# Splitting one x load, dropping ten filler matmuls and moving one transpose to another PSUM bank in a 2:4-sparse matmul on one core

## The chip, the cores and the metric

The kernel runs on one core of a Trainium2 chip. Its time is the device time of one execution in microseconds (us). Three executions of the kernel before took 232.72, 232.92 and 232.72 us, median 232.72 us. A profiled execution beside them took 232.79 us.

The engines named below are TensorE (PE, with its weight loads shown as PEld), VectorE (DVE), ScalarE (ACT), GpSimd (POOL), and SyncE (SP), which here only issues DMAs. ACT issues DMAs as well.

## The reference

```python
B, S, D = 16, 512, 1024              # x: [B,S,D], w: [D,D], b: [D], all bf16
wg = w.reshape(D // 4, 4, D)         # groups of four rows
mag = abs(wg)
thr = second largest of the four magnitudes, per group and column
wp = (wg * (mag >= thr)).reshape(D, D)
return einsum("bsd,df->bsf", x, wp) + b
```

Of every four neighbouring rows of a weight column, only the two largest magnitudes are kept. Then 8192 tokens of 1024 features are multiplied with the pruned 1024x1024 weights and a bias is added.

## The kernel before

**Tiles.** The 8192 tokens are 64 tiles of 128. Tiles 0 to 6 are "packed" tiles (`NPK = 7`): their first half of the features is loaded as it lies in memory (`load_x`, lines 107 to 112), transposed on PE (`transpose`, line 197, instructions on line 202), copied out of PSUM by ACT (`copy_xt`, line 205, token `C`), and multiplied with pieces of the pruned weights as soon as each piece is ready (`mm_piece`, line 221, instructions on line 236, token `M`). All other tiles come through transposing DMAs (lines 118, 244, 416) and use whole pruned weights (`nat`, line 248, instructions on line 250).

**Pruning.** The weights are pruned in six pieces. Piece 0 is 256 columns of the upper half of the rows. It arrives in two loads, one on SP's queue and one on ACT's, and DVE makes it in fifteen instructions from `abs0a` to `mult0h` before further ones follow. The first product `M5.0g` needs the transposed and copied tile 5 (`C5a`) and the first 128 columns of half of piece 0 (`mult0g`).

**Order.** Nothing at the start is left to a scheduler. The loads are issued in the order of lines 124 to 136. The work of PE, DVE, ACT and SP is four lists of tokens (lines 274 to 296), which `run` writes out, each engine in exactly its own list's order. On PE the list starts `T5a T3a T4a F4 T6a M5.0g M3.0g M5.0h M3.0h M4.0g M4.0h T2a`: transposes of tiles 5, 3, 4, four filler matmuls, the transpose of tile 6, six short groups of products, the transpose of tile 2. A little later come `T0a` and `T1a`.

**Fillers.** `filler` (line 143, instructions on line 145) writes matmuls of constant ones into a bank that nobody reads. Lines 409 and 410 put six of 512 columns and fourteen of 128 columns ahead of everything on PE.

**Banks.** PSUM has eight banks: two in `psum_t`, six in `psum_o`. Transposes use the two of `psum_t` in turn, so a transpose waits for the ACT copy of the last but one (`needs`, line 317). Tile 4 alone is transposed in a bank of `psum_o` and waits for no copy. The fillers' bank is also one of `psum_o`.

**Queues and semaphores.** The DMAs get eight semaphores in turn, so a DMA waits until the one eight places before it has landed. SP's queue before: half of piece 0, x tiles 3 and 4 in one load of 256 KB, piece 1, x tile 2, x tiles 0 and 1, piece 2, piece 3, piece 4, then the transposing load `xlead` of tiles 7 to 11, and then the spreads of pruned weights (`wp_nat`). ACT's queue: the other half of piece 0, x tile 5, x tile 6.

**End.** The last `LATE = 6` tiles (58 to 63) store their two halves separately; the last one stores four parts.

Of the kernel before, what the change touches and what calls it, by code (L numbers as in the profile page):

```python
# [10 lines left out]
def kernel(  # L11
# [8 lines left out]
    P = 128  # L20
    bf16 = mybir.dt.bfloat16
    fp32 = mybir.dt.float32
# [10 lines left out]
    FH = 512  # L33
# [8 lines left out]
    STG = 8  # L42
    SOLO = 6
    GROUPS = ((0, 3), (3, 6), (6, 7))
    LATE = 6
    sizes = (4, 8, 8, 8, 8, 8, 8)
    batches = []
    t0 = NPK + LEAD
# [11 lines left out]
    psum_t = ctx.enter_context(tc.tile_pool(name="psum_t", bufs=2, space=bass.MemoryType.PSUM))  # L60
    psum_o = ctx.enter_context(tc.tile_pool(name="psum_o", bufs=6, space=bass.MemoryType.PSUM))
# [12 lines left out]
    def pe(i):  # L74
        return seq("pe", i)
# [4 lines left out]
    def act(i):  # L80
        return seq("act", i)

    def sp(i):
        return seq("sp", i)
# [10 lines left out]
    def tokens(dram, t):  # L95
        a, b_ = next(s for s in GROUPS if s[0] <= t < s[1])
        return dram[a * P:b_ * P].rearrange("(p t) k -> p t k", p=P), t - a
    bias_sb = const.tile([P, Dout], bf16)

    def issue(eng, out_, in_):  # L100
        q = nc.sync if eng == "sp" else nc.scalar
        return seq(eng, q.dma_start(out_, in_))  # L102

    def load_w(g, c0, c1, ma=0, mb=4, eng="sp"):
        issue(eng, w_sb[:, g, ma:mb, c0:c1], wv[:, g, ma:mb, c0:c1])

    def load_x(ta, tb, eng="sp"):
        xs = const.tile([P, tb - ta, HK], bf16, name=f"x_{ta}")
        xv, n = tokens(xf, ta)
        issue(eng, xs[:], xv[:, n:n + tb - ta, :HK])  # L110
        for t in range(ta, tb):
            x_sb[t] = xs[:, t - ta, :]
# [13 lines left out]
    load_x(5, 6, "act")  # L126
    load_x(SOLO, SOLO + 1, "act")
    act(nc.scalar.activation(spark[:], nc.const_aps.tensor(1.0, [P, 1], bf16), Act.Abs))
    load_x(3, 5)
    load_w(0, 256, 512)  # L130
    load_x(2, 3)
    load_x(0, 2)
# [10 lines left out]
    def filler(n, rep=1):  # L143
        for _ in range(n):
            pe(nc.tensor.matmul(warm_ps[:, :rep * P], lhsT=nc.const_aps.tensor(1.0, [P, P], bf16),  # L145
                                rhs=nc.const_aps.tensor(1.0, [P, rep * P], bf16), start=True, stop=True))
# [4 lines left out]
    def spread(g, c0, c1, ks=range(4), eng="sp"):  # L151
        for k in ks:
            issue(eng, wp_nat[:, 4 * g + k, c0:c1], wp[32 * k:32 * k + 32, g, :, c0:c1])
# [39 lines left out]
                self.tt(wp[:, self.g, ms, self.c0 + ca:self.c0 + cb], self.w[:, ms, ca:cb], self.mag[:, ms, ca:cb], Alu.mult)  # L193

    xpk = {}

    def transpose(t):
        xg = x_sb[t].rearrange("p (q m) -> p m q", m=4)
        bank = psum_o.tile([P, FH], fp32, name="ps") if t == 4 else psum_t.tile([P, FH], fp32, name="tp")
        tp = bank[:].bitcast(bf16)[:, :FH].rearrange("p (m q) -> p m q", m=4)  # L200
        for m in range(4):
            pe(nc.tensor.transpose(tp[:, m, :], xg[:, m, :], ident[:]))  # L202
        xpk[t] = tp
# [49 lines left out]
    def open_solo(h):  # L253
        ps = ps_open[(NPK, "h", h)] = psum_t.tile([P, FH], fp32, name="tp")
        nat(xnat[NPK], ps[:], h * FH, (h + 1) * FH, 0, 4, last=3)
# [11 lines left out]
    def stage(key):  # L267
        solo = key[1] == "h"
        q, h, at = (pair_of[key[0]], key[2], int(key[0] != SOLO)) if solo else (key[0], key[1] // 2, key[1] % 2)
        if (q, h) not in staged:  # L270
# [2 lines left out]

    order = {
# [28 lines left out]
    def all_of(tok, i):  # L303
        return [tok + x for x in halves.get(i, ("",))]

    def split_tok(tok):
        k = tok[-1] if tok[-1] in "xyabuvstghjk" else ""
        return (tok[:-1] if k else tok), k

    transposed = []  # L310

    def needs(eng, tok):
        base, k = split_tok(tok)
        if tok[0] == "C":
            return ["T" + tok[1:]]
        if tok[0] == "T":
            return ["C" + transposed[-2]] if tok != "T4a" and len(transposed) > 1 else []
        if tok[0] == "F":
            return []
        if tok[0] == "W":  # L320
            g, h = map(int, tok[1:4].split("."))
            return [n for i, pc in enumerate(pieces) if pc[0] == g and pc[1] // FH == h for n in all_of(f"mult{i}", i)]
        if tok[0] in "XYZ":
            return ["A0h1"] if tok == "Y1" else []
        if tok[0] == "A":
            return ["X0", f"W0.{tok.split('h')[1]}"] + ([f"U{NPK}h{tok[-1]}"] if tok[1] == "3" else [])
        if tok[0] == "E":
            return ["X0", f"W0.{tok[1]}"]
        if tok[0] == "U":
            t, h = map(int, tok[1:].split("h"))  # L330
            if t == NPK:
                return [f"E{h}"]
            return [f"M{t}.{x}" for i, pc in enumerate(pieces) if pc[0] == 0 and pc[1] // FH == h for x in all_of(str(i), i)]
        if base[0] == "M":
            t, i = base[1:].split(".")
            return [f"C{t}a", f"mult{i}{k}"]
        if tok[0] == "S":
            q, n = map(int, tok[1:].split("b"))
            return [f"M{t}.{x}" for i, pc in enumerate(pieces) if pc[0] == 0 and pc[1] // CW == n
                    for t in pairs[q] for x in all_of(str(i), i)]  # L340
        i, step = base[-1], base[:-1]
        before = {"abs": [], "hi": ["abs"], "lo": ["abs"], "t1": ["hi"], "t2": ["lo"],
                  "thr": ["t1", "t2"], "mask": ["thr", "hi", "lo"], "mult": ["mask"]}[step]
        out_ = []
        for b_ in before:
            if b_ in ("t1", "thr") and int(i) in SPLIT:
                out_ += [b_ + i + s for s in {"j": "j", "k": "k", "g": "j", "h": "k"}.get(k, "jk")]
            elif b_ == "t2":
                out_.append(b_ + i)
            elif b_ in ("abs", "hi", "lo") and int(i) in by_rows:  # L350
                out_ += [b_ + i + k] if step in ("hi", "lo") else [b_ + i + s for s in "ab"]
            else:
                out_.append(b_ + i + (k if b_ == "mask" else ""))
        return out_

    def emit(eng, tok):
        base, k = split_tok(tok)
        if tok[0] == "T":
            transpose(int(tok[1:-1]))
            if tok != "T4a":  # L360
                transposed.append(tok[1:])
        elif tok[0] == "F":
            filler(int(tok[1:]))
        elif tok[0] == "W":
            g, h = map(int, tok[1:4].split("."))
            spread(g, h * FH, (h + 1) * FH, {"": range(4), "p": range(2), "q": range(2, 4)}[tok[4:]], eng)
        elif tok[0] == "Z":
            load_w(1, 512, 1024)
            sp(nc.sync.dma_start(bias_sb[:], b.partition_broadcast(P)))
        elif tok[0] == "X":  # L370
            xnat.update(load_lead(int(tok[1:])))
        elif tok[0] == "Y":
            xnat.update(load_low(int(tok[1:])))
            if tok == "Y1":
                tc.add_manual_dep(tails["sp"].ins, ends["A0h1"].ins.name, SYNC, reason="let the spread of the lower weights pass")
        elif tok[0] == "E":
            open_solo(int(tok[1:]))
        elif tok[0] == "U":
            t, h = map(int, tok[1:].split("h"))
            stage((t, "h", h))  # L380
        elif tok[0] == "A":
            open_nat(*map(int, tok[1:].split("h")))
            ends[tok] = tails["pe"]
        elif tok[0] == "C":
            copy_xt(int(tok[1:-1]))
        elif tok[0] == "M":
            mm_piece(*map(int, base[1:].split(".")), part[k], cols.get(k))
        elif tok[0] == "S":
            stage(tuple(map(int, tok[1:].split("b"))))
        else:  # L390
            i = int(base[-1])
            if i not in p:
                p[i] = Piece(i)
            if eng == "act":
                p[i].abs_act()
            else:
                p[i].do(base[:-1], part.get(k, slice(0, 4)), half.get(k, slice(0, 2)), cols.get(k))
# [9 lines left out]
            assert moved, queues  # L407

    filler(6, 4)
    filler(14)  # L410
    run({eng: order[eng].split() for eng in order})

    def load_nat(ta, tb):
# [39 lines left out]
    def store(eng, t, o, c0=0, c1=Dout):  # L453
        issue(eng, rows(t)[:, c0:c1], o[:, c0:c1])
# [25 lines left out]
    for bi, (tb, nb) in enumerate(batches):  # L480
        if bi:
            load_batch(bi + 1)
        for j in range(nb):
            t = tb + j
            xt = xnat[t]
            o = outp.tile([P, Dout], bf16, name="o")
            if t == NT - 1:
                for n, (c0, c1) in enumerate(((0, FH), (FH, FH + CW), (FH + CW, Dout - P), (Dout - P, Dout))):
                    ps = psum_o.tile([P, FH], fp32, name="ps")
# [3 lines left out]
            else:  # L493
# [4 lines left out]
                for h in range(2):  # L498
                    evac(o, pss[h][:], h * FH, (h + 1) * FH)
                    if t >= NT - LATE:  # L500
                        store("act", t, o, h * FH, (h + 1) * FH)
                if t < NT - LATE:
                    store("act", t, o)
# [30 lines left out]
```

## Time and profile before

| | |
|---|---|
| median of three runs | 232.72 us |
| profiled execution | 232.79 us, span 231.0 us |
| PE busy | 226.1 us (98%) |
| PE busy from 6.29 to 19.39 us (products with pieces) | 13.10 of 13.10 us |
| PE idle ahead of its first transpose | 0.38 us, until x tile 5 is there |
| DVE idle ahead of its first instruction | 3.58 us, until the first weights are there |
| fillers (line 145) | 24 instructions |
| transposes on PE (line 202) | 28 instructions |
| mean traffic of the DMAs from 4.95 to 6.29 us | 346 GB/s, share of the 16 engines 1.11 |

Times are counted from the span's start. In the timeline a row merges instructions of one line that follow one another: start, length, engine, line, operation, output and inputs, number, and in brackets the idle time ahead of it with what ended it. The length of a matmul row runs to the end of the last matmul's passage through the array; the next matmul starts well before that. The chain of waits goes back from the last instruction, each step to what released it.

### The profile page before, as it was taken

What the parts mean: (1) busy time and instruction counts of PE and PEld (TensorE: products, weight loads), DVE (VectorE), ACT (ScalarE), POOL (GpSimd) and SP (SyncE); (2) the same over time, 40 slices, a digit from 0 to 9 for tenths busy, and PEclk for the clock granted to TensorE, in tenths of its full rate; (3) what the DMA queues carried; (4) which work ended last, traced back from release to release, by engine and by line L of the source; (5) the groups of instructions that cost most, each with busy time, mean ns of one, the idle gap of its engine ahead of it and who ended that gap; (6) DMA issues with size and microseconds to landing.
All of it is one profiled execution on the core that took longest, in us unless ns stands there. A gap on an engine that the chain in (4) does not pass through costs nothing.

```text
span 231.0 us, 2846 instructions
## 1 busy us (share of the span) xinstructions
PE 226.1 (98%) x1142; PEld 110.9 (48%) x1162; DVE 107.8 (47%) x196; ACT 13.3 (6%) x26; POOL 17.6 (8%) x15
## 2 busy tenths in 40 slices
PE   7999999999999999999999999999999999999995
PEld 4985444444444444444444444444444444444443
DVE  3999787844424424424424424423423423433434
ACT  3665100000000000000000000000000000000000
POOL 1000199700000000000000000000000000000000
PEclk9999999999999999999999999999999999999999
DMA  6999799997399222991159821796129952122122
GB/s 210 296 216 238 190 208 224 290 282 266 134 239 272 82 91 72 229 287 69 72 125 236 229 94 71 144 255 197 63 91 198 219 176 84 53 91 91 54 85 91
DMA packets 79292, 38.19 MB, mean 165 GB/s; under 512 B 64176, under 2 KB 71728, under 8 KB 79280
## 3 DMA queue, kind: packets, MB, share of 16 engines
q1 hardware_dynamic: 68352, 20.75, 44.2%
q10 hardware_dynamic: 10928, 17.27, 21.3%
q8 instruction: 9, 0.15, 0.3%
q14 instruction: 3, 0.02, 0.0%
HBM read 3.28 MB, written 16.78 MB: 87 GB/s over the span
## 4 chain that ended last, share of the span: by engine, by line
PE 96%; DMA 2%; issue 1%; ACTq 0%; DVE 0%
PE ps L250 88%; PE ps L236 5%; PE tp L250 2%; DMA x<-in_x_dram 2%; PE tp L202 1%; ACTq L102 0%; DVE o L442 0%; PE ps L145 0%; PE ps L202 0%
## 5 line engine op out<-in xcount | busy, mean ns | idle before, releaser
L250 PE MATMUL ps<-wp_nat,xb 128*128 128x512 bf16 (+1 forms) x831 | 178.9, 375 | 0.9
L250 PEld LDWEIGHTS <-xb 128*128 128x128 bf16 x848 | 82.4, 98 | 97.5
L442 DVE TENSOR_TENSOR o<-ps,bias_sb 128x512 bf16<-128x512 f32 (+1 forms) x112 | 71.6, 677 | 113.7 <-PE ps L250 111.4
L438 POOL TENSOR_TENSOR st<-st,bias_sb 128x1024 f32<-128x1024 f32 x8 | 16.7, 2122 | 0.0
L250 PE MATMUL ps<-wp_nat,xlead 128*128 128x512 bf16 x63 | 14.7, 379 | 0.1
L250 PEld LDWEIGHTS <-xlead 128*128 128x128 bf16 x88 | 8.6, 98 | 10.2
L236 PE MATMUL ps<-wp,xt 128*128 128x256 bf16 (+1 forms) x126 | 12.9, 261 | 0.0
L444 DVE TENSOR_TENSOR o<-ps,st 128x512 bf16<-128x512 f32 x16 | 11.1, 692 | 2.8 <-PE ps L250 2.2
L236 PEld LDWEIGHTS <-xt 128*128 128x128 bf16 x126 | 11.2, 98 | 1.2
L250 PE MATMUL ps<-wp_nat,xlow 128*128 128x512 bf16 x47 | 10.6, 379 | 0.1
L272 ACT COPY st<-ps 128x512 f32<-128x512 f32 x14 | 7.4, 594 | 3.0 <-PE ps L236 3.0
L250 PEld LDWEIGHTS <-xlow 128*128 128x128 bf16 x48 | 5.0, 103 | 5.4
L166 DVE TENSOR_TENSOR wp<-w_sb,mag 128x256 bf16<-128x256 bf16 (+2 forms) x13 | 6.2, 483 | 0.1
L166 DVE TENSOR_TENSOR mag<-mag,hi 128x256 bf16<-128x256 bf16 (+2 forms) x13 | 6.0, 484 | 0.1
L250 PE MATMUL tp<-wp_nat,xlead 128*128 128x512 bf16 x23 | 5.8, 379 | 0.0
L145 PE MATMUL ps<-const-bfloat16-1.0 128*128 128x128 bf16 (+1 forms) x24 | 4.2, 345 | 0.8 <-PEq L518 0.8
L177 DVE TENSOR_SCALAR mag<-w_sb 128x512 uint16<-128x512 uint16 (+2 forms) x6 | 2.7, 467 | 3.6 <-DMA w_sb<-in_w_dram 3.6
L145 PEld LDWEIGHTS <-const-bfloat16-1.0 128*128 128x128 bf16 x24 | 2.3, 124 | 2.4 <-issue 2.4
L166 DVE TENSOR_TENSOR hi<-mag 128x512 bf16<-128x512 bf16 (+2 forms) x7 | 3.2, 459 | 0.0
L166 DVE TENSOR_TENSOR lo<-mag 128x512 bf16<-128x512 bf16 (+2 forms) x7 | 3.1, 458 | 0.0
L202 PE MATMUL tp<-ident,x 128*128 128x128 bf16 x24 | 2.1, 220 | 0.4 <-DMA x<-in_x_dram 0.4
L207 ACT COPY xt<-tp 128x256 f32<-128x256 f32 x6 | 2.1, 374 | 2.6 <-PE tp L202 2.6
(18 smaller groups left out, 15.0 us busy)
## 6 DMA issues: line engine op xcount, KB each, us to landing
out_dram<-o ACTq DMA_DIRECT2D x58, 256.0 KB, 2.5
wp_nat<-wp SPq DMA_DIRECT2D x14, 128.0 KB, 3.3
out_dram<-o ACTq DMA_DIRECT2D x10, 128.0 KB, 1.7
w_sb<-in_w_dram SPq DMA_DIRECT2D x2, 512.0 KB, 4.6
w_sb<-in_w_dram SPq DMA_DIRECT2D x3, 256.0 KB, 4.6
x<-in_x_dram SPq DMA_DIRECT2D x2, 256.0 KB, 4.0
x<-in_x_dram ACTq DMA_DIRECT2D x2, 128.0 KB, 3.6
bias_sb<-in_b_dram SPq DMA_DIRECT2D x1, 256.0 KB, 4.7
```

The lines of the kernel that those rows point to most:

```text
L145: pe(nc.tensor.matmul(warm_ps[:, :rep * P], lhsT=nc.const_aps.tensor(1.0, [P, P], bf16), rhs=nc.const_aps.tensor(1.0, [P, rep * P], bf16), ...
L166: dve(nc.vector.tensor_tensor(out, a, b_, op=op))
L177: dve(nc.vector.tensor_single_scalar(self.mag[:, ms, :].bitcast(u16), self.w[:, ms, :].bitcast(u16), 0x7FFF, op=Alu.bitwise_and))
L202: pe(nc.tensor.transpose(tp[:, m, :], xg[:, m, :], ident[:]))
L207: act(nc.scalar.copy(xt[:].bitcast(fp32), xpk[t].bitcast(fp32)))
L236: pe(nc.tensor.matmul(ps[:, c0 + ca + d:c0 + cb + d], lhsT=xpk[t][:, m, :], rhs=wp[:, g, m, c0 + ca:c0 + cb], start=(new and m == ms.start ...
L250: pe(nc.tensor.matmul(ps, lhsT=xt[:, kt - koff, :], rhs=wp_nat[:, kt, c0:c1], start=(kt == first), stop=(kt == last)))
L272: act(nc.scalar.copy(staged[(q, h)][:, at, :, :].rearrange("p t c -> p (t c)"), ps_open.pop(key)[:]))
L438: pool(nc.gpsimd.tensor_tensor(st[:], st[:], bias.to_broadcast([P, 2, 2, CW]), op=Alu.add))
L442: dve(nc.vector.tensor_tensor(o[:, c0:c1], ps, bias_sb[:, c0:c1], op=Alu.add))
L444: dve(nc.vector.tensor_tensor(o[:, c0:c1].rearrange("p (n c) -> p n c", n=2), ps.rearrange("p (n c) -> p n c", n=2), add, op=Alu.add))
```

## The change

1. x tiles 3 and 4 come in two loads of 128 KB on SP's queue instead of one of 256 KB. SP's queue has one DMA more ahead of piece 1.
2. Fourteen short fillers ahead of the transposes become eight. The six long ones stay.
3. The four fillers `F4` between the transposes of tiles 4 and 6 go.
4. Tile 6, like tile 4, is transposed in a bank of `psum_o`. Its transpose waits for no copy, and the later transposes count back over tiles 5, 3, 2, 0, 1 only: tile 2 waits for the copy of tile 5 and tile 0 for that of tile 3.
5. `LATE` goes from 6 to 5: tile 58 is stored in one piece of 256 KB instead of two of 128 KB. The program has as many DMAs as before; those between the split load and this store use the next semaphore in the ring.

```diff
-    LATE = 6
+    LATE = 5
...
-    load_x(3, 5)
+    load_x(3, 4)
+    load_x(4, 5)
     load_w(0, 256, 512)
...
+    LOOSE = (4, 6)
...
-        bank = psum_o.tile([P, FH], fp32, name="ps") if t == 4 else psum_t.tile([P, FH], fp32, name="tp")
+        bank = psum_o.tile([P, FH], fp32, name="ps") if t in LOOSE else psum_t.tile([P, FH], fp32, name="tp")
...
-            "T5a T3a T4a F4 T6a M5.0g M3.0g M5.0h M3.0h M4.0g M4.0h T2a M6.0h M3.0u M6.0u M5.0u T0a M4.0u T1a "
+            "T5a T3a T4a T6a M5.0g M3.0g M5.0h M3.0h M4.0g M4.0h T2a M6.0h M3.0u M6.0u M5.0u T0a M4.0u T1a "
...
-            return ["C" + transposed[-2]] if tok != "T4a" and len(transposed) > 1 else []
+            return ["C" + transposed[-2]] if int(tok[1:-1]) not in LOOSE and len(transposed) > 1 else []
...
-            if tok != "T4a":
+            if int(tok[1:-1]) not in LOOSE:
                 transposed.append(tok[1:])
...
     filler(6, 4)
-    filler(14)
+    filler(8)
```

## The prediction

> **What bounds the kernel now.** I read the engines' busy time first, then the busy time by stretches, then the chain of waits over the first microseconds, and last the timeline where the chain meets PE's first product. The page's first part and the stretches:
>
> ```profile
> PE 226.1 (98%) x1142; PEld 110.9 (48%) x1162; DVE 107.8 (47%) x196; ACT 13.3 (6%) x26; POOL 17.6 (8%) x15
> ...
> 6.29:19.39 13.10, 13.10 (x139) 11.95 (x139) 12.83 (x42) 9.08 (x19) 0.00 (x0) 1.00 1.01 251
> ```
>
> PE is the bound. From 6.29 us, its first product, to 19.39 us it is busy in every instant (second and third number of the stretch), and the chain of waits goes on over PE alone to 228.4 us. The last store and the closing take the rest of the span. So the end is 6.29 us plus a fixed amount of PE work plus a fixed tail. An edit pays only if it brings the first product forward, removes PE work behind it, or shortens the tail; it costs if it opens a gap behind 6.29 us or moves that product back. The chain for the head:
>
> ```profile
> 1.26 3.64 DMA x<-in_x_dram
> 4.90 0.05 issue
> 4.95 0.64 PE tp L202 x8
> 5.59 0.22 PE ps L202 x4
> 5.81 0.23 PE ps L145 x4
> 6.04 0.22 PE tp L202 x4
> 6.27 0.03 issue
> 6.29 0.83 PE ps L236 x12
> ```
>
> Read like this, x tile 5 (issued at 1.26 us, landed at 4.90) starts the transposes, the four fillers of L145 take 0.23 us of the path, and their removal gains 0.23 us. The timeline says otherwise:
>
> ```profile
> 3.58 0.50 DVE L177 TENSOR_SCALAR mag<-w_sb 128x512 uint16<-128x512 uint16 x2 [3.58 <-DMA w_sb<-in_w_dram]
> ...
> 5.88 0.38 PE L202 MATMUL tp<-ident,x 128*128 128x128 bf16 x4
> ...
> 5.95 0.49 DVE L166 TENSOR_TENSOR wp<-w_sb,mag 128x256 bf16<-128x256 bf16 x2
> ...
> 6.29 0.83 PE L236 MATMUL ps<-wp,xt 128*128 128x128 bf16 x12
> ```
>
> The row at 5.95 is the pair `mult0g` and `mult0h`; one takes 0.29 us, so `mult0g`, which the first product needs, ends at 6.24, and the product starts 0.05 us later. PE's row at 5.88 holds four transposes that follow one another every 0.056 us (0.22 us for four in the chain), so PE could take the next matmul at 5.88 + 4 x 0.056 = 6.10; that the row reaches to 6.26 is the passage of the last one through the array. PE therefore waits for DVE from 6.10 to 6.29. DVE has no gap from 3.58 to there, so the first product hangs on the landing of the first weights (issued 0.73, landed 2.8 us later) and the fourteen instructions from `abs0a` to `mult0g`.
>
> **The change, part by part.**
>
> *Fillers 14 to 8.* The short fillers follow one another every 0.107 us up to 3.93 and every 0.057 us from 4.00 on. The eighth starts at 4.00, so the block now ends its issue at about 4.06 instead of 4.41. PE's next instruction waits for x tile 5 until 4.95 either way. Path: 0, covered by that load; without the cover it would be a gain of 6 x 0.057 = 0.34 us, never a loss by itself.
>
> *F4 out, tile 6 in a product bank.* Tile 6's transposes move from 5.88 to 5.65. Tile 6's load allows it: issued at 1.79, 3.6 us to land, 5.4. Its old wait was for the copy of tile 5 (ACT 5.40, 0.37 long, so 5.78); behind F4 it cost nothing, without F4 it would have cost 5.83 − 5.65 = 0.18 us, so the two edits belong together. PE then is free at 5.88 and waits for `mult0g` 0.41 us instead of 0.19. Path: 0; what covers it is DVE's chain. If DVE were not late the gain would be 0.22 us, and that is the lower end. The other transposes' waits become older ones: tile 2 at 6.96 waits for the copy of tile 5 (done 5.78), tile 0 at 7.62 for that of tile 3 (done by 6.06), tile 1 as before for tile 2's. The product bank of tile 6 is wanted again by a group behind 9 us, its copy is done by 6.7. All 0.
>
> *x tiles 3 and 4 apart.* PE's list has tile 5 first, so an earlier tile 3 starts nothing: PE reaches it at 5.17, and the joint load has landed at 1.24 + 3.7 = 4.94. Gain 0. The cost sits on SP's queue, which gets one more issue. The queue before:
>
> ```profile
> 0.73 0.45 SPq L102 DMA_DIRECT2D w_sb<-in_w_dram  x1
> 1.24 0.46 SPq L102 DMA_DIRECT2D x<-in_x_dram  x1
> 1.75 0.68 SPq L102 DMA_DIRECT2D w_sb<-in_w_dram  x1
> 2.46 1.08 SPq L102 DMA_DIRECT2D x<-in_x_dram  x2
> 3.75 1.91 SPq L102 DMA_DIRECT2D w_sb<-in_w_dram  x3
> 5.71 5.14 SPq L118 DMA_TRANSPOSE xlead<-in_x_dram  x1
> ```
>
> One issue is 1.75 − 1.24 = 0.51 us. Piece 1 goes from 1.75 to 2.26, x tile 2 from 2.47 to 2.98, and x tiles 0 and 1 from 3.12 to about 3.77: 3.63 by the shift, but by the ring of eight semaphores this load now waits for the second half of piece 0 (0.73 + 3.0 = 3.73). Who waits for them: DVE reads piece 1 at 6.56 (landed 1.75 + 4.5 = 6.25), PE tile 2 at 6.91 (landed 2.47 + 4.2 = 6.67), PE tile 0 at 7.51 (landed 3.12 + 4.3 = 7.42). Margins 0.31, 0.24 and 0.09 us. Does the issue's delay reach the landing? The first weights land 2.8 us after issue, these three 4.2 to 4.5 us, with the DMA engines' share at 1.1 in those stretches: 1.4 us and more of each is standing in the queue behind bytes that the change neither adds to nor reorders. A shift of 0.5 to 0.65 disappears in that. Path: 0 taken, nearer to the rows than the other end, at which the whole shift arrives: tile 0 lands at 8.07, and PE, in strict order, stands 8.07 − 7.51 = 0.56 us. Gain below nothing is excluded for these loads, since nobody waits for them now.
>
> Behind them, pieces 2 and 3 move to about 4.4 and 5.0 and the transposing load to about 6.3. That load's issue takes 5.14 us for 640 tokens, a later one 3.44 us for 768, so about 2.3 us (5.14 − 3.44 x 640/768) of it is waiting for room in the queue, estimated from these two rows; it should end near 10.85 as before. If not, the spreads start 0.5 us later: the last of the first four is issued at 13.79 and lands about 3.3 us later at most, and PE first reads them at 19.2; SP itself waits 0.8 us for DVE at 16.56 and is in step again there. 0.
>
> *LATE 5.* Tile 58's store happens near 212 us; stores of 256 KB land in 2.0 us there, 128 KB in 1.7. The end waits for the stores issued at 227 to 229. 0.
>
> *Sum:* 0 on the path. The span stays 231.0 us, the profiled execution took 232.79 (1.8 us lie around the span), 0.07 above the median 232.72. Forecast: **232.7 us**, own range 232.5 to 232.9.
>
> **The rivals.**
>
> *The slow pitch stays (slower).* PE's matmuls run at half pace at first: long fillers start every 0.43 us (rows at 2.43 and 2.86), later products of 512 columns follow every 0.22. The pace changes at 3.93 to 4.00, 3.2 us after the first filler, though the profile's granted clock reads 1.00 throughout. The new block of fillers ends its issue only about 0.06 us behind that moment and leaves PE idle to 4.95, 0.9 us instead of 0.5. If the change of pace depends on uninterrupted work and comes a little later in other executions, it misses the block. Price, if it then takes 3.2 us from 4.95 again: sixteen transposes at 0.107 end at 6.66, twelve short products at 7.95, and at 8.15 PE stands where it stood at 7.07: +1.08, 233.8 us. If it comes one stretch of 3.2 us after 3.94, at 7.14, four or five short products are done and PE stands where it stood at 6.55: +0.59, 233.3. It decides once the pace changes later than about 5.7 us, when PE's half-pace transposes outlast DVE. Against it: up to 3.94 the work is the same as before, and the four times shown lie within 0.2 us, so the moment hardly wanders.
>
> [...]
>
> *The loads come late (slower).* The 0.56 us above, 233.3 us. For it: the margin of tile 0 is 0.09 us. Against it: the standing time of 1.4 us.
>
> *The chain is right (faster).* F4's 0.23 us come off: 232.5 us. For it: the chain's own rows. Against it: `mult0g` at 6.24. It stays inside what a measurement of this kernel can tell from no change, about 0.2% or 0.47 us.
>
> **How the numbers follow.** Forecast 0.60; slow pitch 0.20; late loads 0.08; chain 0.06; 0.06 for what I don't see, half of it slower and half faster by more than 0.2%. Same: forecast and chain, 0.66. Slower: 0.31. Faster: 0.03. The range goes from 232.4, below the chain's case, to 233.4, which takes in the late loads and the cheaper end of the slow pitch, and leaves out its dearer end.
>
> **What the profile after would show.** Right: tile 6's transposes at about 5.65, PE idle from 5.88, the first product at 6.29, PE without a gap behind it. Slow pitch: transposes every 0.107 us at 5 us. Late loads: PE idle ahead of tile 0's transposes near 7.6. Chain: the first product at 6.07. A first weight landing elsewhere than at 3.58 would move everything and make the forecast wrong in either direction.

## The result, and the profile after

| | before | after |
|---|---|---|
| executions side by side | 7 | 7 |
| median | 232.79 us (232.67 to 233.08) | 233.44 us (233.18 to 233.89) |
| ratio, 95% interval | | 1.0024 [1.0014, 1.0034] |
| profiled execution, span | 232.79 us, 231.0 us | 233.18 us, 231.4 us |

The kernel became slower by 0.24%, 0.65 us by the medians and 0.39 us by the pair of profiled executions. The forecast was 232.7 us, no change; the time lies 0.04 us above the upper end of the range, 233.4 us. The profiled execution of the kernel after is the fastest of its seven, so the account from its profile covers 0.39 us of the loss and not all of the 0.65.

The page of the kernel after, its first part (busy time of each engine):

```profile
PE 227.1 (98%) x1152; PEld 110.4 (48%) x1152; DVE 107.9 (47%) x196; ACT 13.3 (6%) x26; POOL 17.6 (8%) x15
```

PE issues ten matmuls less: 1152 against the 1162 weight loads of before, whose own matmul records are short of twenty, so that its 226.1 us can't be set against this 227.1. PE is still the bound with 98%, and the reading goes to its start. The chain of waits of the kernel after (start, length, what), from the load that it now hangs on:

```profile
1.75 4.16 DMA x<-in_x_dram
5.91 0.05 issue
5.95 0.64 PE ps L204 x8
6.59 0.67 PE ps L238 x12
7.26 0.35 PE tp L204 x4
7.61 0.44 PE ps L238 x5
8.05 0.32 PE tp L204 x4
```

The load issued at 1.75 us is x tile 4's own, and it lands at 5.91. Before, tiles 3 and 4 came together and both had landed at 4.96. (Times of landing are those at which a load's last semaphore update came.) The timeline of the kernel after says who waits for it and for the loads behind it:

```profile
1.24 0.93 SPq L102 DMA_DIRECT2D x<-in_x_dram  x2
...
2.21 0.67 SPq L102 DMA_DIRECT2D w_sb<-in_w_dram  x1
...
2.92 1.21 SPq L102 DMA_DIRECT2D x<-in_x_dram  x2
...
4.47 0.81 PE L204 MATMUL tp<-ident,x 128*128 128x128 bf16 x8
...
5.93 0.48 DVE L167 TENSOR_TENSOR wp<-w_sb,mag 128x256 bf16<-128x256 bf16 x2
...
5.95 0.64 PE L204 MATMUL ps<-ident,x 128*128 128x128 bf16 x8 [0.68 <-DMA x<-in_x_dram]
...
6.13 5.24 SPq L118 DMA_TRANSPOSE xlead<-in_x_dram  x1
...
6.43 0.83 PE L238 MATMUL ps<-wp,xt 128*128 128x128 bf16 x12
...
6.81 0.43 DVE L178 TENSOR_SCALAR mag<-w_sb 128x1024 uint16<-128x1024 uint16 x1 [0.19 <-DMA w_sb<-in_w_dram]
...
7.20 0.41 PE L204 MATMUL tp<-ident,x 128*128 128x128 bf16 x4
...
7.95 0.26 PEld L204 LDWEIGHTS <-x 128*128 128x128 bf16 x4 [0.18 <-DMA x<-in_x_dram]
```

The split does bring something forward: tile 3 lands at 4.09 and tile 5, on ACT's queue, at 4.42 instead of 4.90, so PE does tiles 5 and 3 from 4.47 on instead of 4.95. But then it stands 0.68 us for tile 4, and the gain is lost. Tiles 4 and 6 follow in one row at 5.95, and 5.95 + 8 x 0.056 = 6.40. `mult0g`, the first of the pair at 5.93 and 0.29 us long, is done at 6.22. So the first product at 6.43 waits for the transposes and no longer for DVE: +0.14 us against 6.29. The rows at 7.20 and 7.95 are tiles 2 and 0, 0.24 and 0.33 us later than before; their loads landed at 7.15 and 7.91, just ahead. Piece 1 holds DVE for 0.19 us at 6.81. Three landings thus cost PE 0.14, 0.10 and 0.09 us. From tile 1's transposes on, 0.35 us later than before, everything runs as it did, and the span is longer by about the same, 0.4 us.

The landings on SP's queue moved as the issues did. Issue and landing in the two profiles:

| load | issued before | landed | from issue | issued after | landed | from issue |
|---|---|---|---|---|---|---|
| piece 1 (256 KB) | 1.75 | 6.26 | 4.5 | 2.21 | 6.79 | 4.6 |
| x tile 2 (128 KB) | 2.46 | 6.64 | 4.2 | 2.93 | 7.15 | 4.2 |
| x tiles 0 and 1 (256 KB) | 3.11 | 7.42 | 4.3 | 3.76 | 7.91 | 4.1 |
| x tile 6 (128 KB, ACT's queue) | 1.78 | 5.44 | 3.7 | 1.78 | 6.12 | 4.3 |

Tile 6's load is issued on the other queue and as early as before, and it too lands 0.68 us later, just ahead of the moment at which PE wants it (5.95 + 4 x 0.056 = 6.17). The traffic of the DMAs while these loads are under way is lower in this pair, not equal. Busy time by stretches of half a microsecond; the last two columns are the share of the 16 DMA engines and GB/s. Before:

```profile
4.00:4.50 0.50, 0.50 (x10) 0.39 (x7) 0.50 (x4) 0.00 (x0) 0.00 (x0) 1.00 1.11 328
4.50:5.00 0.50, 0.12 (x3) 0.06 (x2) 0.50 (x3) 0.00 (x0) 0.00 (x0) 1.00 1.09 321
5.00:5.50 0.50, 0.50 (x10) 0.50 (x11) 0.50 (x5) 0.10 (x1) 0.00 (x0) 1.00 1.14 345
```

After:

```profile
4.00:4.50 0.50, 0.38 (x5) 0.11 (x3) 0.50 (x4) 0.00 (x0) 0.00 (x0) 1.00 0.65 189
4.50:5.00 0.50, 0.50 (x6) 0.50 (x7) 0.50 (x4) 0.00 (x0) 0.00 (x0) 1.00 0.87 261
5.00:5.50 0.50, 0.28 (x5) 0.12 (x2) 0.50 (x5) 0.41 (x2) 0.00 (x0) 1.00 0.91 260
```

These three stretches move 497 KB before and 355 KB after. The missing 142 KB are 0.43 us at the rate before (331 GB/s), most of the 0.5 us by which the landings are late. At a share of 0.65 the engines have room, so it is not for want of room that the loads are late.

### The profile page after: what moved, and what is told of

Same layout as the page of the kernel before. It is cut to its first block, busy times and chain, and to the rows that moved or that the text cites. A ratio compares the mean times of both kernels' runs of the same rounds, so it can differ in the third digit from the quotient of the medians.

```text
span 231.4 us, 2845 instructions
## 1 busy us (share of the span) xinstructions
PE 227.1 (98%) x1152; PEld 110.4 (48%) x1152; DVE 107.9 (47%) x196; ACT 13.3 (6%) x26; POOL 17.6 (8%) x15
## 4 chain that ended last, share of the span: by engine, by line
PE 96%; DMA 2%; SPq 0%; DVE 0%; issue 0%
PE ps L252 88%; PE ps L238 5%; PE tp L252 2%; DMA x<-in_x_dram 2%; SPq L102 0%; PE tp L204 0%; PE ps L204 0%; DVE o L444 0%
## 5 line engine op out<-in xcount | busy, mean ns | idle before, releaser
L252 PE MATMUL ps<-wp_nat,xb 128*128 128x512 bf16 (+2 forms) x848 | 179.8, 375 | 0.0
L146 PE MATMUL ps<-const-bfloat16-1.0 128*128 128x128 bf16 (+1 forms) x14 | 3.6, 445 | 0.8 <-PEq L520 0.8
L146 PEld LDWEIGHTS <-const-bfloat16-1.0 128*128 128x128 bf16 x14 | 1.7, 141 | 2.4 <-issue 2.4
L204 PEld LDWEIGHTS <-x 128*128 128x128 bf16 x28 | 2.0, 119 | 1.5 <-DMA x<-in_x_dram 1.4
```

The costliest lines, as they stand in the source:

```text
L252: pe(nc.tensor.matmul(ps, lhsT=xt[:, kt - koff, :], rhs=wp_nat[:, kt, c0:c1], start=(kt == first), stop=(kt == last)))
```

## The experiments

All ratios are against the kernel before on the same chip in the same set of runs. "T4" and "T0" are the transposes of tiles 4 and 0.

**First set: which part costs?** The split alone, all but the split, the change with its fillers left as they were, and the shorter block of fillers alone.

```diff
 # the split alone (on the kernel before)
-    load_x(3, 5)
+    load_x(3, 4)
+    load_x(4, 5)
 # all but the split (on the kernel after)
-    load_x(3, 4)
-    load_x(4, 5)
+    load_x(3, 5)
 # fourteen fillers (on the kernel after)
-    filler(8)
+    filler(14)
 # eight fillers alone (on the kernel before)
-    filler(14)
+    filler(8)
```

The split alone:

> The kernel before with the one edit that x tiles 3 and 4 come in two loads; all fillers, the bank of tile 6 and the stores as before. Theory A, queue: one more DMA on SP's queue makes every later load on it land about 0.5 us later (piece 1 near 6.8 us, x tile 2 near 7.15, x tiles 0 and 1 near 7.9) and tile 4 near 5.9 instead of 4.96. PE then stands ahead of tile 4, and with F4 still behind tile 4 the first product comes at about 6.65: the time is 0.4 to 0.7 us above before. Theory B, slow pitch: the fillers are those of before, so the time is that of before within 0.1 us.

All but the split:

> The changed kernel with the joint load of x tiles 3 and 4 put back; eight short fillers, no F4, tile 6 in a product bank and LATE 5 stay. Theory A: the loads land as in the kernel before, the first product is at 6.29 us and the time is that of before within 0.1 us. Theory B: the short block of fillers is left, so the time stays 0.4 to 0.7 us above before, with the transposes following one another every 0.107 us for a while.

The change with fourteen fillers:

> The changed kernel with fourteen short fillers ahead of the transposes again; the split load, the missing F4, tile 6's bank and LATE 5 stay. Theory A: tile 4 still lands near 5.9 us, the time is 0.4 to 0.65 us above before, as for the changed kernel. Theory B: the time falls to that of before.

Eight fillers alone:

> The kernel before with eight short fillers instead of fourteen and nothing else changed. Theory A: no difference from before beyond 0.1 us. Theory B: 0.3 to 0.7 us above before, and PE's matmuls after 4.95 us follow one another every 0.107 us until the pace changes.

| kernel | median us (range, n) | ratio [95%] | T4, T0 start | span |
|---|---|---|---|---|
| before | 232.87 (30) | | 5.42, 7.62 | 231.0 |
| split alone | 233.78 (233.29–234.56, 8) | 1.0034 [1.0019, 1.0050] | 5.72, 8.25 | 231.8 |
| all but the split | 232.91 (232.73–235.02, 11) | 1.0005 [0.9988, 1.0022] | 5.69, 7.55 | 231.0 |
| fourteen fillers | 233.26 (232.91–234.24, 11) | 1.0021 [1.0011, 1.0031] | 5.80, 8.62 | 232.0 |
| eight fillers alone | 232.82 (232.71–233.20, 11) | 1.0001 [0.9992, 1.0010] | –, 7.69 | 231.1 |

The loss comes and goes with the split. Timeline of the split alone (T4 and T0):

```profile
5.72 0.41 PE L203 MATMUL ps<-ident,x 128*128 128x128 bf16 x4 [0.18 <-DMA x<-in_x_dram]
...
8.25 0.41 PE L203 MATMUL tp<-ident,x 128*128 128x128 bf16 x4 [0.28 <-DMA x<-in_x_dram]
```

Timeline of the change with fourteen fillers (T4, T2):

```profile
5.80 0.64 PE L204 MATMUL ps<-ident,x 128*128 128x128 bf16 x8 [0.75 <-DMA x<-in_x_dram]
...
7.82 0.41 PE L204 MATMUL tp<-ident,x 128*128 128x128 bf16 x4 [0.72 <-DMA x<-in_x_dram]
```

Both wait for loads where the kernel before did not, however many fillers there are. In the three profiles with the split, x tiles 0 and 1 land at 7.91, 8.20 and 8.57, which is a spread of 0.66 us between executions of nearly the same queue. Their spans, 231.4, 231.8 and 232.0 us, rise with it, which fits the larger loss of the medians; the executions without a profile can't be followed.

The half pace does not explain the loss. Timeline of all but the split (tiles 5 and 3, tiles 4 and 6, first product, T0):

```profile
4.89 0.96 PE L203 MATMUL tp<-ident,x 128*128 128x128 bf16 x8 [0.55 <-DMA x<-in_x_dram]
...
5.69 0.61 PE L203 MATMUL ps<-ident,x 128*128 128x128 bf16 x8
...
6.18 0.87 PE L237 MATMUL ps<-wp,xt 128*128 128x128 bf16 x12
...
7.55 0.39 PE L203 MATMUL tp<-ident,x 128*128 128x128 bf16 x4
```

From 4.89 to 5.69 the eight transposes follow one another every 0.1 us, so the pace changed at about 5.6 us here and not at 3.9. The first product starts at 6.18 all the same, 0.05 us after DVE's `mult0g` (5.84 + 0.29 = 6.13). One of the eleven executions of this kernel took 235.02 us, the others at most 232.98; it has no profile, so a pace that came later still is not excluded for it.

Eight fillers alone show the second limit. Timeline (first product, T0):

```profile
6.14 0.83 PE L236 MATMUL ps<-wp,xt 128*128 128x128 bf16 x12
...
7.69 0.41 PE L202 MATMUL tp<-ident,x 128*128 128x128 bf16 x4
```

DVE started earlier in this execution and the first product came at 6.14, 0.15 us before its time, yet T0 is 0.07 us later than in the kernel before, because x tiles 0 and 1 landed at 7.65. The kernel before stands on two bounds of nearly the same length: DVE's chain to the first product, and the landing of the last x tiles.

**Second set: is it the place in SP's queue, the number of loads, or the bytes?** A load of 16 KB that nobody reads is put into the kernel before, once on SP's queue behind tiles 3 and 4, once on ACT's between tiles 5 and 6. In a third kernel the change's tile 4 goes to ACT's queue behind tile 6. A fourth takes all fillers out of the kernel before. The "common generator" of the expectations is a conjecture of mine: no run shows such a part, only when the loads land.

```diff
 # small load on SP's queue, behind load_x(3, 5)
+    scr = const.tile([P, 64], bf16, name="scr")
+    issue("sp", scr[:], w[0:P, 0:64])
 # the same on ACT's queue, behind load_x(5, 6, "act")
+    issue("act", scr[:], w[0:P, 0:64])
 # tile 4 on ACT (on the kernel after)
+    load_x(4, 5, "act")
...
-    load_x(4, 5)
 # no fillers (on the kernel before; F4 goes out of PE's list as well)
-    filler(6, 4)
-    filler(14)
```

The small load on SP's queue:

> The kernel before, with one load more on SP's queue behind x tiles 3 and 4: 16 KB of the weights into a tile that nobody reads. x tiles 3 and 4 stay in one load. Theory A1, SP's pace: loads arrive a fixed time after their issue, whatever their size, so a load without bytes to speak of delays every later load of SP's queue by one issue, 0.4 to 0.5 us (x tiles 0 and 1 land near 7.9), tile 4 lands as before near 4.95, and the time is 0.2 to 0.5 us above before. Theory A2, common generator: the same here. Theory A3, bytes: loads stand behind bytes, 16 KB are 0.05 us, landings and time as before within 0.1 us.

The small load on ACT's queue:

> The kernel before, with the same load of 16 KB on ACT's queue between x tiles 5 and 6. Theory A1: SP's loads land as before, only x tile 6 comes 0.5 us later (near 5.9, the first product near 6.5), time 0 to 0.3 us above before. Theory A2: what turns the loads of both queues into packets works on one load after the other, so piece 1 and x tiles 2, 0 and 1 land 0.4 to 0.5 us later as in the run with the load on SP's queue, time 0.3 to 0.6 us above before. Theory A3: as before within 0.1 us.

Tile 4 on ACT's queue:

> The changed kernel with the load of x tile 4 on ACT's queue behind x tile 6 instead of on SP's. SP's queue then has as many loads as before the change. Theory A1: piece 1 and x tiles 2, 0 and 1 land as in the kernel before or earlier (x tiles 0 and 1 by 7.4), tile 4 lands near 6.0, and the time is 0.1 to 0.3 us above before, from tile 4 alone. Theory A2: the number of loads is what counts; x tiles 0 and 1 still land 0.4 us and more later than before, and the time is 0.4 to 0.7 us above before.

No fillers:

> The kernel before without any filler: neither the six long ones nor the fourteen short ones nor F4. The loads are those of before. If the pace of PE's matmuls changes only some 3 us after PE's first work, the transposes and the first products run every 0.107 us until about 8 us, and the time is 0.6 to 1.1 us above before. If the pace at the start costs nothing because DVE and the loads are later, the time is that of before within 0.1 us.

| kernel | median us (range, n) | ratio [95%] | span |
|---|---|---|---|
| before | 232.80 (18) | | 231.0 |
| small load on SP | 233.46 (232.88–234.52, 9) | 1.0025 [1.0006, 1.0045] | 231.9 |
| small load on ACT | 233.55 (233.38–234.48, 8) | 1.0037 [1.0024, 1.0049] | 231.8 |
| tile 4 on ACT | 234.28 (233.47–235.57, 8) | 1.0064 [1.0039, 1.0090] | 233.5 |
| no fillers | 234.37 (233.75–234.99, 6) | 1.0066 [1.0050, 1.0081] | 232.5 |

A load of 16 KB costs what the split costs, on either queue. Of the small load on SP's queue, the DMA issues (output and input, queue, operation, count, KB, us from issue to landing) are

```profile
x<-in_x_dram SPq DMA_DIRECT2D x1, 256.0 KB, 4.7
w_sb<-in_w_dram SPq DMA_DIRECT2D x1, 256.0 KB, 4.5
...
scr<-in_w_dram SPq DMA_DIRECT2D x1, 16.0 KB, 3.5
```

and T0 starts at 8.37 after an idle time of 0.34 us. Piece 1 keeps its 4.5 us from an issue that is one place later. The small load on ACT's queue, DMA issues:

```profile
w_sb<-in_w_dram SPq DMA_DIRECT2D x1, 256.0 KB, 5.3
...
x<-in_x_dram SPq DMA_DIRECT2D x1, 128.0 KB, 4.9
...
scr<-in_w_dram ACTq DMA_DIRECT2D x1, 16.0 KB, 4.0
```

Its timeline, SP's third issue and ACT's third issue:

```profile
1.75 0.68 SPq L102 DMA_DIRECT2D w_sb<-in_w_dram  x1
1.78 0.45 ACTq L102 DMA_DIRECT2D scr<-in_w_dram  x1
```

And its stretch from 4.0 to 4.5 us:

```profile
4.00:4.50 0.50, 0.50 (x8) 0.50 (x6) 0.50 (x4) 0.24 (x2) 0.00 (x0) 1.00 0.46 109
```

SP issues piece 1 at 1.75 as before, up to x tile 2 nothing on its queue has moved, and still piece 1 takes 5.3 us instead of 4.5 and x tile 2 takes 4.9 instead of 4.2. So it is not only SP's issue that must be early: one more load on the other queue delays them as well, while the DMA engines run at 109 GB/s in that half microsecond.

One profile is one execution, so the spread matters. Four kernels have the first loads of before (before, all but the split, eight fillers alone, no fillers); in their profiles piece 1 lands at 6.26 to 6.50 us, x tile 2 at 6.64 to 6.87 and x tiles 0 and 1 at 7.42 to 7.65. In the five with one load more (after, split alone, fourteen fillers, the two small loads) they land at 6.56 to 7.03, 7.07 to 7.77 and 7.91 to 8.57. The two groups do not overlap, and the kernel before is the earliest of its group. The traffic separates them less well: from 4.0 to 4.5 us it is 222 to 328 GB/s in the first group and 109 to 265 in the second.

The 5.3 us instead of 4.5 speak against two queues that are independent of one another. The 16 KB themselves, 0.05 us at 328 GB/s, do not account for the delay.

Moving tile 4 to ACT's queue therefore does not repair the split, and it shows something else. Timeline of tile 4 on ACT (tiles 4 and 6, first product):

```profile
6.68 1.04 PE L204 MATMUL ps<-ident,x 128*128 128x128 bf16 x8 [1.24 <-DMA x<-in_x_dram]
7.52 1.48 PE L238 MATMUL ps<-wp,xt 128*128 128x128 bf16 x12
```

Twelve products take 1.48 us instead of 0.83: PE is still at half pace at 8 us. The eight executions form two groups of four, 233.47 to 233.66 and 234.90 to 235.57, and the profile is one of the second, so the median, 1.5 us above before where at most 0.7 was expected, lies between them. Whether the first group had the full pace in time no profile shows. Without fillers the same half pace is in the timeline (tiles 5 and 3, first product, T0):

```profile
4.72 1.04 PE L202 MATMUL tp<-ident,x 128*128 128x128 bf16 x8 [4.72 <-DMA x<-in_x_dram]
...
6.41 1.48 PE L236 MATMUL ps<-wp,xt 128*128 128x128 bf16 x12
...
8.97 0.57 PE L202 MATMUL tp<-ident,x 128*128 128x128 bf16 x4
```

It loses 8.97 − 7.62 = 1.35 us by T0, and 1.5 us of time, more than the 0.6 to 1.1 I had expected. The fillers are worth that much, and the pace is a real cost; it is only not the cost of this change.

**Third set: can fewer loads gain?** Tiles 3, 4 and 5 in one load on SP's queue; the second kernel also puts tile 2 on ACT's queue. Both also take the change's other parts (eight fillers, no `F4`, tile 6 in a product bank, `LATE` 5).

```diff
 # on the kernel after
-    load_x(5, 6, "act")
...
-    load_x(3, 4)
-    load_x(4, 5)
+    load_x(3, 6)
 # second kernel, further
+    load_x(2, 3, "act")
...
-    load_x(2, 3)
```

One load for three tiles:

> The changed kernel with x tiles 3, 4 and 5 in one load of 384 KB on SP's queue: two loads fewer than the changed kernel, one fewer than the kernel before. If each load costs the common generator about half a microsecond whatever its size, piece 1 and x tiles 2, 0 and 1 land as early as in the kernel before or up to 0.4 us earlier, tiles 3 to 5 land near 4.9, no transpose waits after that, and the time is that of before or 0.1 to 0.3 us below it. If bytes are what counts, landings and time are those of the changed kernel, 0.2% above before.

The same with tile 2 on ACT's queue:

> As the run with x tiles 3, 4 and 5 in one load, and x tile 2 on ACT's queue behind x tile 6, so that SP issues x tiles 0 and 1 at about 2.5 us. Common generator: the number of loads is the same, tile 2 comes earlier and piece 1 about as late as it takes one load, so PE's wait moves to the first products of piece 1 if anywhere; time within 0.2 us of the run with tile 2 on SP's queue. If SP's own pace mattered, x tiles 0 and 1 land 0.5 us earlier and the time is 0.1 to 0.3 us below before.

The first took 235.78 us (233.48 to 236.58, 12), ratio 1.0081 [1.0050, 1.0113], again in two groups (five up to 234.24, seven from 235.68). The second took 236.48 us (235.97 to 237.09, 6), ratio 1.0134 [1.0105, 1.0162]. Of my two expectations for the first, one had it no slower and the other 0.2% slower; it is slower than both. Timeline of the first, the load and the first transposes:

```profile
1.24 0.67 SPq L102 DMA_DIRECT2D x<-in_x_dram  x1
...
6.22 0.64 PE L202 MATMUL tp<-ident,x 128*128 128x128 bf16 x8 [1.88 <-DMA x<-in_x_dram]
```

The three tiles land at 6.18, 4.9 us after issue, where two took 3.7. Everything behind them is late too (piece 1 6.95, x tiles 0 and 1 8.14), although there is one load fewer. The profile is one of the faster group, 233.96 us; what the slower seven executions met it does not show. So "the fewer loads, the sooner" is not the whole rule, and why a load of three tiles is so late stays open.

The second is 0.7 us slower than the first, where I had expected at most 0.2. There the load of three tiles lands at 7.48, 6.2 us after its issue, and PE idles longest. Timeline:

```profile
7.53 1.04 PE L202 MATMUL tp<-ident,x 128*128 128x128 bf16 x8 [3.40 <-DMA x<-in_x_dram]
```

Stretches (the third number from the end is the granted clock):

```profile
7.00:7.50 0.50, 0.00 (x0) 0.00 (x0) 0.00 (x0) 0.00 (x0) 0.00 (x0) 0.66 1.09 347
8.00:10.00 2.00, 2.00 (x22) 2.00 (x20) 1.63 (x7) 1.49 (x4) 0.00 (x0) 0.50 1.12 314
10.00:12.00 2.00, 2.00 (x30) 1.98 (x29) 2.00 (x9) 0.75 (x3) 0.00 (x0) 0.86 1.22 255
```

PE's work had ended at 7.53 − 3.40 = 4.13. The mean of 0.66 puts the fall to 0.50 at 7.16, after 3.03 us without work, and the mean of 0.86 puts the return at 10.56, after 3.03 us of work.

**Fourth set: bytes or load?** In the kernel before, tile 6's load is cut from 128 to 16 KB, or left out; tile 6's products then use tile 5's features.

```diff
 # 16 KB instead of 128
-    load_x(SOLO, SOLO + 1, "act")
+    scr = const.tile([P, 64], bf16, name="scr")
+    issue("act", scr[:], xf[SOLO * P:NPK * P, 0:64])
+    x_sb[SOLO] = x_sb[5]
 # no load: without the scr lines
```

A load of 16 KB:

> The kernel before with x tile 6's load on ACT's queue cut from 128 KB to 16 KB that nobody reads; tile 6's transpose takes tile 5's data instead, so the first half of tile 6's features is wrong. As many loads as before, 112 KB fewer bytes (about 0.33 us at the 340 GB/s of that stretch). If the number of loads sets the landings: piece 1 and x tiles 2, 0 and 1 land as in the kernel before (6.26, 6.64, 7.42 us), within 0.1. If bytes set them: 0.3 us earlier (5.95, 6.3, 7.1).

No load:

> As the run with 16 KB, but without that load at all; tile 6's transpose takes tile 5's data, so the first half of tile 6's features is wrong. If the number of loads sets the landings: piece 1 and x tiles 2, 0 and 1 land 0.4 us earlier than in the run with 16 KB. If bytes set them: as in the run with 16 KB within 0.1 us. The time falls by at most 0.2 us in both, because DVE's chain to the first product stays.

| kernel | median us (range, n) | ratio [95%] | piece 1, x tile 2, x tiles 0 and 1 landed |
|---|---|---|---|
| before | 232.99 (19) | | 6.26, 6.64, 7.42 |
| 16 KB | 232.76 (232.54–233.07, 10) | 0.9992 [0.9982, 1.0003] | 6.26, 6.62, 7.39 |
| no load | 233.14 (232.66–234.18, 10) | 1.0007 [0.9992, 1.0022] | 6.13, 6.50, 7.21 |

112 KB less change no landing by more than 0.03 us, where 0.33 us were expected if bytes set them. The stretch of the kernel with 16 KB shows that nothing else took the place of these bytes:

```profile
4.00:4.50 0.50, 0.50 (x10) 0.40 (x7) 0.50 (x4) 0.00 (x0) 0.00 (x0) 1.00 0.69 180
```

The whole load less brings the landings 0.13 to 0.18 us forward against the kernel with 16 KB. That is less than half of the 0.4 us I expected, and within the 0.24 us by which profiles of the same queue differ. With one profile each, the result speaks against bytes as the only thing that sets the landings; a gain from the load left out is not shown. With the load out, the DMA issues read

```profile
x<-in_x_dram SPq DMA_DIRECT2D x1, 256.0 KB, 4.1
...
x<-in_x_dram SPq DMA_DIRECT2D x1, 128.0 KB, 4.0
```

so the time from issue hardly falls below the 4.2 and 4.3 of before. Removing a load gave back at most 0.2 us in these profiles; adding one put the three landings 0.3 to 1.15 us behind those of before. Neither kernel leaves the measurement's reach of no change. No kernel that I ran is faster than the kernel before.

## Why the prediction was wrong

**The step that failed** is the fate of SP's later issues: "1.4 us and more of each is standing in the queue behind bytes that the change neither adds to nor reorders. A shift of 0.5 to 0.65 disappears in that. Path: 0 taken". I had taken the difference of two lags, 4.2 and 2.8 us, for slack. The shifts of 0.47, 0.46 and 0.65 at issue arrived as 0.53, 0.51 and 0.49 at landing. The lag is not a stand behind bytes alone: cutting 112 KB out of the traffic left it as it was, within 0.03 us, and 16 KB more on the other queue lengthened it, from 4.5 to 5.3 us for piece 1. A hint was in the profile before: three loads of 256, 128 and 256 KB, issued within 1.4 us, had nearly the same lag, 4.2 to 4.5.

The bytes still count behind piece 1. In the kernel before, x tile 2 lands 0.38 us after piece 1 and x tiles 0 and 1 another 0.78 us later, and 128 and 256 KB at about 340 GB/s take just that; in the kernel after the distances are 0.36 and 0.76. So a queue behind bytes is there, but all of it comes 0.5 us later. The prediction's argument needs DMA engines that stay full until these loads have their turn; in the profile after their share falls to 0.65, 0.87 and 0.91 between 4.0 and 5.5 us.

**A missing term.** I worked out the split's gain for tile 3 and never asked when tile 4 would land by itself. In the joint load it landed at 4.96; alone, in the next place of the queue, it landed at 5.91 and was the first to stop PE, by 0.68 us. This cost 0.14 of the 0.33 us by T0, and it is the reason that DVE's chain no longer set the first product. Nor did I ask whether ACT's queue would notice: tile 6, "3.6 us to land, 5.4", landed at 6.12, just early enough to cost nothing.

**The rival that came true** is the late loads. I priced it at 0.56 us; the profile shows 0.39 us, the medians 0.65. Its 0.56 came from tile 0 alone, where the profile has three waits, of which each takes up part of the next, so that it comes so near is partly luck. Its mechanism, later loads with the shift in full, was right for two of the three waits; the first, tile 4's, it did not have. Its chance of 0.08 was too low, and the margins beside it (0.31, 0.24, 0.09 us) were there to say so: any shift of 0.5 exceeds all three.

**The slow pitch** was not it. Its deciding point, "later than about 5.7 us", is borne out by a pace change at about 5.6 that cost nothing. Its counterargument, that the moment "hardly wanders", was wrong: in the profiles it lies anywhere from 3.6 to 4.1, at 4.9, 5.1, 5.4 and 5.6, and at 9 to 10 in the kernel with tile 4 on ACT's queue and in the one without fillers. In the kernel after it lies at about 4.9, and PE waits for tile 4 until 5.95 anyway. That this rival's cheaper price of +0.59, 233.3 us, lies close to the measured 233.44 is chance: all but the split has the same fillers and measures 1.0005. How long a block of work must be for the full pace is not shown: 3.03 us of work brought the full clock back in the second kernel of the third set, while in the profile of the kernel after the block of fillers, 3.57 us long, ended at half pace.

**The chain's reading** (0.23 us gain from `F4`) fell: all but the split measures 1.0005. Its interval, [0.9988, 1.0022], would just admit 0.23 us, but in its profile the first product starts right behind `mult0g`, at 6.18.

**What was right at 0.** The fillers (1.0001 alone), and `F4`, tile 6's bank and `LATE` together with them (1.0005). The lower end, 0.22 us of gain, stayed out as argued: DVE's chain covered it.

**The transposing load.** It was to end at 10.85 whatever its start, with 2.3 us of its issue a wait for room. It takes 5.24 us from 6.13 and ends at 11.37, so none of the shift is absorbed, and the wait for room, my estimate, is not shown. As the fallback said, it is harmless: the spreads begin at 11.50 instead of 10.97 and PE has no wait where it first reads them.

What stays open is what lies between issue and landing. The runs show that an added load on either queue makes the later loads of both late (0.3 to 1.15 us on SP's queue in five profiles, 0.68 us for x tile 6 on ACT's in the kernel after), even where it brings only 16 KB, and no gain from removing one. They do not show the part of the chip that does this, nor why three tiles in one load fare worse than two.

## What to carry to other kernels

In a burst of loads at a kernel's start, do not take a long lag from issue to landing for slack that absorbs a later issue. Carry the shift to the landing in full and compare it with the margin of the one who waits; here shifts of 0.46 to 0.65 us arrived as 0.3 to 1.15 us. Splitting a load in this burst brought the first half and ACT's load beside it forward (4.09 instead of 4.96 us and 4.42 instead of 4.90), but added a load for all that followed, on both queues, and the second half landed 0.7 to 0.95 us later than the joint load had. When a first product waits for one engine by 0.2 us, list the next two waits with their margins as well, since a kernel tuned like this one stands on several bounds at once.

## What the runs showed of the hardware that I had not expected

- A load of 16 KB on ACT's queue delayed a load on SP's queue that was issued at the same time as before by 0.5 to 0.8 us (5.3 us from issue to landing instead of 4.5 to 4.8 in the four kernels with the loads of before), with the DMA engines' traffic down to 109 GB/s for half a microsecond.
- 384 KB in one load landed 4.9 us after issue, and 6.2 us in another kernel; 256 KB in the same place took 3.5 to 3.7 us.
- PE's pace changed anywhere from 3.6 to 5.6 us in most kernels with fillers, at 10 us in one of them and at 9 us without fillers, while the column of the granted clock reads 1.00. In these first microseconds it showed the half rate, 0.50, only where PE had idled 3.03 us after the pace was up.
